# Eight token blocks instead of seven in the first feed-forward layer: 2, 2, 2, 3, 3, 4, 4, 4 chunks for 2, 2, 4, 4, 4, 4, 4

## The chip, the cores and the metric

The kernel runs on one core of one Trainium2 chip. The metric is the device time of one execution in microseconds, and the number quoted for a kernel is the median of several runs. Engines are named as in the profile: PE is the matmul engine and PEld its weight loads, DVE the vector engine, ACT the scalar engine, POOL GpSimd, SP the queue that issues the transfers.

## What is computed

A chunked linear-attention layer (4 batches, 8 heads, 768 positions, head dimension 32, state 16), then two feed-forward layers on the 3072 resulting tokens of width 256:

```python
y   = linear_attention(x, a, B, C)                 # a decaying state is carried along the positions
x1  = (sigmoid(y @ w_gate) * (y @ w_val)) @ w_out  # d_ff 1536: "layer 1"
h   = x1 @ w2_in                                   # d_ff 2048: "layer 2"
out = (h * sigmoid(h)) @ w2_out
```

All arrays are float32.

## The kernel before, in words

**Chunks.** The positions are cut into chunks of 128: six for each batch, 24 in all, numbered 0 to 23. One attention chunk `q` goes through the following steps. The loads `at_load_bc` (L265, L266), `at_load_x` (L273) and `at_loadL` (L252: 512 KB of decays, broadcast out of the small DRAM copy `ac_d`) are issued by SP. `at_bc1`, `at_bc2` and `at_bc3` split B and C in three bf16 parts and transpose them by DMA (L327). `at_L` is one long DVE scan over the decays (L338). `at_cb` multiplies C with B on PE (L381) and masks the product into `L` on DVE (L383). `at_y` makes the chunk's output in PSUM: four matmuls from the carried state (L392, none for the first chunk of a batch) and sixteen small ones (L398). `at_bw`, `at_cwT`, `at_state` and `at_state2` carry the state on (L346, L360, L414, L423, L435). `at_yT` writes the chunk into the block's input as a high part `xT0` (ACT, L450) and a low part `xT1` (DVE, L451). `y` has one PSUM buffer, `x` three buffers, `L` four, and each `xT` tile two. `slot_steps(s)` lists these steps for a slot `s`: the output of chunk `s`, the products of chunk `s + 1`, the preparation of chunk `s + 2` and the loads of chunk `s + 3`.

**Blocks and ticks.** Layer 1 takes the tokens in blocks of the chunks listed in `BLOCKS`; a block of `n` chunks is a moving operand of 128 `n` columns (256 for two chunks, 512 for four). A tick is a pair of a block and one of the twelve slices `f` of d_ff. A tick has six matmuls for the gate and six for the value (`three`, L509: two halves of the contraction by three products of high and low parts), a sigmoid out of PSUM on ACT (L522), the product out of PSUM on DVE (L530), the split into `gh` (ACT, L503) and `gl` (DVE, L539), and, two ticks later (`LAG`), six matmuls of `m1_out` (L558) that accumulate into `acc`. The gate and value products share three PSUM buffers (`gv`). At the end of a block `acc` is copied to `x1T` by two ACT copies (L569). Blocks 0 and 1 use the first seven `w_out` slices unsplit and have fewer, slower output matmuls there.

**Order.** Blocks 0 and 1 run interleaved, in groups of three slices, while the weights of layer 1 arrive and are split (`conv`). Their 24 ticks also work through a list of attention steps: all of what block 1 still needs, and the slots that fill block 2. From block 2 on the ticks are block by block, and the ticks of block `b` carry the slots of the chunks of block `b + 1`:

```python
ast += slots(ends[1] - 3, ends[1], ends[1], NQ) + slots(ends[1], ends[2], 0, NQ)
...
if b + 1 < len(BLOCKS):
    steps += [g for s in range(ends[b], ends[b + 1]) for g in slot_steps(s)]
    if b == 4:
        extra = w2_steps(0, NA)      # first weights of layer 2
```

`RUNS` and `WPOS` say how many of these steps stand before, between and behind the gate and the value of each of the 24 first ticks, and where the weight steps stand in the list. From block 2 on, a tick takes `rate` steps at each of three places, with `rate = -(-len(steps) // 32)`. SP issues its transfers in the order of the program. On the other engines the order is set when the kernel is built: the tile framework takes, by a simulated clock, the first instruction in program order that is ready. At run time each engine works through its own list in order.

**Where each chunk's block input lives.** Block 2 writes into the `xT` buffers of block 0, so that its first chunk (4) can be written only after the last gate and value of block 0 in slice 11; chunk 5's output waits for chunk 4's PSUM buffer, and so on.

Of the kernel before, what the change touches and what calls it, by code (L numbers as in the profile page):

```python
# [17 lines left out]
U32 = mybir.dt.uint32  # L18


BLOCKS = [2, 2, 4, 4, 4, 4, 4]
LAG = 2

NX = 4
# [21 lines left out]
def tile_linattn_moe_moe(  # L46
# [36 lines left out]
    U = nb * H  # L83
    assert sum(BLOCKS) == NQ and H * N == P and DM == 2 * P

# [131 lines left out]
    def w1_split(f0, f1):  # L217

        for f in range(f0, f1):
            hi, lo = w1[:, f, 0, 2 * DM :], w1[:, f, 1, 2 * DM :]  # L220
            nc.scalar.copy(hi, whole(f))
            nc.vector.tensor_sub(lo, whole(f), hi.bitcast(F32))
# [12 lines left out]
    blk_of = []  # L235
    for b, n in enumerate(BLOCKS):
        for i in range(n):
# [259 lines left out]
    g1 = {}  # L497
    start_of = [sum(BLOCKS[:b]) * L for b in range(len(BLOCKS))]

# [14 lines left out]
    def m1_gate(b, f):  # L514
        n = BLOCKS[b] * L
        ps = ps_gv.tile([P, 512], F32, tag="gv", name=f"g{b}_{f}", bufs=GV)
        three(ps, w1[:, f], 0, xT[b], n)
        if b < 2 and f < NAT:
            sg = gp.tile([P, 512], F32, tag=("gh", "gl")[f % 2], name=f"sg{b}_{f}", bufs=3)
        else:  # L520
            sg = gp.tile([P, 512], F32, tag="sg", name=f"sg{b}_{f}", bufs=2)
        nc.scalar.activation(sg[:, :n], ps[:, :n], AF.Sigmoid)  # L522
        g1[b, f] = [sg]

    def m1_val(b, f):
        n = BLOCKS[b] * L
        ps = ps_gv.tile([P, 512], F32, tag="gv", name=f"v{b}_{f}", bufs=GV)
        three(ps, w1[:, f], DM, xT[b], n)
        sg = g1[b, f][0]
        nc.vector.tensor_mul(sg[:, :n], ps[:, :n], sg[:, :n])  # L530
        if b >= 2 or f >= NAT:
            g1[b, f] += gsplit(f, sg, n, f"{b}_{f}")

    def m1_lo(b, f):
        n = BLOCKS[b] * L
        if len(g1[b, f]) == 1:
            return
        sg, hi, lo = g1[b, f]
        nc.vector.tensor_sub(lo[:, :n], sg[:, :n], hi[:, :n].bitcast(F32))  # L539

    def m1_out(b, f):
        n = BLOCKS[b] * L

        small = n <= 256
        if f == 0 and not (small and b % 2):
            acc[b] = ps_acc.tile([P, KM, 512], F32, tag="acc", name=f"acc{b}")
        a_ = acc[b - b % 2][:, b % 2] if small else acc[b]
        g = g1.pop((b, f))
        w = w1[:, f, :, 2 * DM :]
        if len(g) == 1:  # L550
            terms = ((whole(f), g[0]),)
        else:
            terms = ((w[:, 0], g[1]), (w[:, 0], g[2]), (w[:, 1], g[1]))
        for m in range(KM):
            ms = slice(m * P, (m + 1) * P)
            o = a_[:, m * n : (m + 1) * n] if small else a_[:, m, :n]
            for z, (v, g) in enumerate(terms):
                mm = nc.tensor.matmul(  # L558
                    o, v[:, ms], g[:, :n],
                    start=(f == 0 and z == 0 and not (small and m)),  # L560
                    stop=(f == NF1 - 1 and z == len(terms) - 1), skip_group_check=True,
                )
                if (b, f, m, z) in ZO:
                    pe_last[0] = mm.ins
                    zeros(ZO[b, f, m, z], o, False)
        if f == NF1 - 1:
            for m in range(KM):
                o = a_[:, m * n : (m + 1) * n] if small else a_[:, m, :n]
                x1_end[:] = [nc.scalar.copy(x1T[0][:, m, start_of[b] : start_of[b] + n], o)]  # L569
# [99 lines left out]
    def run(k):  # L669
        for _ in range(min(k, len(steps))):  # L670
            steps.pop(0)()

    def need(k):
        while k not in seen:
            steps.pop(0)()
# [5 lines left out]
    def w2_alloc(key, n):  # L681
        stack, side = (ctx, "left") if key == "a" else (w1stack, "right")
        w2p = stack.enter_context(tc.tile_pool(name=f"w2{key}", bufs=1, side=side))
        w2st[key] = w2p.tile([P, n, 2, 2 * DM], F32R, name=f"w2{key}")
# [13 lines left out]
    for b, f in ticks:  # L698
        if b < 2:
            need(("w", f))  # L700
            need(("x", b))
            z = f // GRP
            if b == 0 and f == z * GRP and z > 1:
                if (z - 2) * GRP < NAT:
                    steps.append(lambda z=z: w1_split((z - 2) * GRP, min((z - 1) * GRP, NAT)))
            if f == 0 and b == 1:
                rate = -(-len(steps) // RT)
        elif f == 0:
            run(len(steps))
            if b == 2:  # L710
                m1_lo(*prev)
                prev = None
                while queue_o:
                    m1_out(*queue_o.pop(0))
                for z in range(max(0, len(GR) - 2), len(GR)):
                    if z * GRP < NAT:
                        steps.append(lambda z=z: w1_split(z * GRP, min((z + 1) * GRP, NAT)))
                run(len(steps))
                sstack.close()
                w2_alloc("a", NA)  # L720
                stg["n"], stg["raw"], stg["cvt"] = 512, 2, 2
                stg["p"] = sstack.enter_context(tc.tile_pool(name="stg2", bufs=1))
            if b + 1 < len(BLOCKS):
                steps += [g for s in range(ends[b], ends[b + 1]) for g in slot_steps(s)]
                if b == 4:
                    extra = w2_steps(0, NA)
                    k = len(steps) // (len(extra) + 1)
                    for z, g in enumerate(extra):
                        steps.insert((z + 1) * (k + 1) - 1, g)
            else:  # L730
                astack.close()
                w2_alloc("b", NF2 - NA)
                held += w2_steps(NA, NF2)
            rate = -(-len(steps) // RT)
        counts = RUNS[ticks.index((b, f))] if b < 2 else [rate] * 3
        if b or f:
            run(counts[0])
        m1_gate(b, f)
        run(counts[1])
        if prev is not None:  # L740
            m1_lo(*prev)
        m1_val(b, f)
        prev = (b, f)
        run(counts[2])
        queue_o.append((b, f))
        if len(queue_o) > LAG:
            m1_out(*queue_o.pop(0))
        if held and f == LAG - 1:

            stg["behind"] = x1_end[0].ins  # L750
            steps += held
            held = []
            rate = -(-len(steps) // (3 * (NF1 - LAG)))
# [149 lines left out]
```

## Time and profile before

| | |
|---|---|
| median of 3 runs | 665.57 us (664.33 to 668.0) |
| the profiled execution, its own time | 663.99 us |
| span of its records | 662.2 us |
| mean granted PE clock | 0.992 of full speed |
| PE busy, weight loads busy | 635.5 us (96%), 522.0 us (79%) |
| DVE, ACT, POOL busy | 432.8 us (65%), 329.0 us (50%), 108.7 us (16%) |

The ends of matmuls are modelled in the trace, and one matmul's record overlaps the next. So a busy PE is not a PE at its peak: the distance from the start of one matmul to the start of the next says what it costs. A row of a timeline gives the start, the time from the start of the first to the end of the last instruction that it merges, and the idle time ahead of it with the instruction that ended it. Layer 1's blocks end, one after the other, with the two copies of L569; the last 264 us are layer 2.

### The profile page before, as it was taken

The page shows a single profiled execution, that of the slowest core. Times are in us where ns is not written, and L with a number is a line of the kernel's source. Part 1 is how long each engine was busy: PE and PEld are TensorE (multiplying, and loading weights), DVE is VectorE, ACT ScalarE, POOL GpSimd, SP SyncE. Part 2 cuts the span into 40 slices and gives each one's busy share as a digit, 9 for nine tenths or more (in the row PEclk, how much of TensorE's full clock was granted, in tenths as well). Part 3 has the DMA queues.
Part 4 walks back from the last instruction along what each step waited for, and adds up shares of the span by engine and source line. Part 5 has one row for each costly group of instructions (what it writes and reads, how often), then busy time and mean ns, then how long its engine had stood idle before and what let it go on. Part 6 is the DMA issues. An engine that isn't in the chain of part 4 may idle for free.

```text
span 662.2 us, 9861 instructions
## 1 busy us (share of the span) xinstructions
PE 635.5 (96%) x3680; PEld 522.0 (79%) x3682; DVE 432.8 (65%) x660; ACT 329.0 (50%) x649; POOL 108.7 (16%) x129
## 2 busy tenths in 40 slices
PE   5788898999999999999999999999999999999998
PEld 2477796777778787787888878888888888888886
DVE  8988987676768578656348885564564655544644
ACT  5675554544544554434336664544554544444543
POOL 4555432211221222311002410000000000000000
PEclk9998999999999999999999999999999999999999
DMA  8958577774656365342002410000000000000000
GB/s 207 267 146 212 89 158 154 153 128 109 120 121 145 77 145 119 81 125 75 0 1 66 157 33 1 1 32 1 1 32 1 1 32 1 33 0 1 33 0 33
DMA packets 140145, 51.18 MB, mean 77 GB/s; under 512 B 119009, under 2 KB 133537, under 8 KB 140097
## 3 DMA queue, kind: packets, MB, share of 16 engines
q1 hardware_dynamic: 139952, 50.41, 32.1%
q8 instruction: 29, 0.48, 0.3%
q14 instruction: 20, 0.16, 0.1%
q10 hardware_dynamic: 144, 0.13, 0.1%
HBM read 36.80 MB, written 3.24 MB: 60 GB/s over the span
## 4 chain that ended last, share of the span: by engine, by line
PE 79%; DVE 4%; DMA 4%; issue 3%; POOL 2%; ACT 1%; SPq 0%; DVEq 0%; POOLq 0%; ACTq 0%
PE h L509 20%; PE o L807 13%; PE v L509 11%; PE acc L558 11%; PE g L509 11%; PE o L828 7%; DMA raw<-in_moe_w_out_dram 3%; PE y L398 2%; DMA L<-ac_d 1%; POOL cvt L185 1%; PE cb L381 1%; PE y L392 1%; DVE sg L530 1%; DVE cvt L178 1%; DVE L L338 1%
## 5 line engine op out<-in xcount | busy, mean ns | idle before, releaser
L509 PE MATMUL v<-xT,w 128*128 128x512 f32 (+1 forms) x504 | 119.4, 369 | 3.9 <-ACT sg L522 2.4
L509 PE MATMUL g<-xT,w 128*128 128x512 f32 (+1 forms) x504 | 120.8, 370 | 0.0
L782 DVE TENSOR_TENSOR sh<-h,sh 128x512 f32<-128x512 f32 x96 | 66.2, 691 | 63.2 <-ACT sh L781 61.7
L509 PE MATMUL h<-x2T,w2b 128*128 128x512 f32 x432 | 107.0, 389 | 0.0
L791 DVE TENSOR_TENSOR gl<-sh,gh 128x512 fp32r<-128x512 f32 x96 | 65.8, 690 | 58.4 <-ACT gh L786 56.9
L509 PEld LDWEIGHTS v<-xT,w 128*128 128x128 f32 x504 | 87.4, 192 | 19.3 <-ACT sg L522 3.0
L509 PEld LDWEIGHTS g<-xT,w 128*128 128x128 f32 x504 | 87.7, 191 | 16.3 <-issue 1.5
L558 PE MATMUL acc<-gh,w 128*128 128x512 f32 (+1 forms) x280 | 94.5, 380 | 0.2 <-ACT x1T L569 0.2
L781 ACT ACTIVATE sh<-h 128x512 f32<-128x512 f32 x96 | 57.5, 599 | 73.3 <-PE h L509 70.2
L509 PEld LDWEIGHTS h<-x2T,w2b 128*128 128x128 f32 x432 | 80.7, 188 | 16.5
L786 ACT CAST gh<-sh 128x512 fp32r<-128x512 f32 x96 | 59.0, 620 | 62.2 <-PE o L807 31.0
L503 ACT CAST gh<-sg 128x512 fp32r<-128x512 f32 (+1 forms) x70 | 41.2, 588 | 93.6 <-DVE sg L530 93.6
L807 PE MATMUL o<-w2b,gh 128*128 128x512 f32 x280 | 74.2, 390 | 0.0
L530 DVE TENSOR_TENSOR sg<-v,sg 128x512 f32<-128x512 f32 (+1 forms) x84 | 50.8, 607 | 30.4 <-PE v L509 29.5
L539 DVE TENSOR_TENSOR gl<-sg,gh 128x512 fp32r<-128x512 f32 (+1 forms) x70 | 50.6, 723 | 23.3 <-ACT gh L503 23.0
L338 DVE TENSOR_TENSOR_SCAN L<-L,eye 128x1024 f32<-128x1024 f32 x24 | 55.2, 2302 | 16.0 <-DMA L<-ac_d 15.9
L185 POOL TENSOR_TENSOR cvt<-cvt,raw 128x512 int32<-128x512 int32 (+1 forms) x28 | 46.5, 1664 | 98.7 <-DVE cvt L178 81.5
L522 ACT ACTIVATE sg<-g 128x512 f32<-128x512 f32 (+1 forms) x84 | 44.8, 534 | 31.5 <-PE g L509 28.6
L558 PEld LDWEIGHTS acc<-gh,w 128*128 128x128 f32 x280 | 52.3, 190 | 9.9 <-ACT x1T L569 0.3
L807 PEld LDWEIGHTS o<-w2b,gh 128*128 128x128 f32 x280 | 51.8, 188 | 10.3
L558 PE MATMUL acc<-gl,w 128*128 128x512 f32 (+1 forms) x140 | 53.3, 380 | 1.0 <-DVE gl L539 1.0
L828 PEld LDWEIGHTS o<-w2b,gl 128*128 128x128 f32 x288 | 36.9, 191 | 1.3
(95 smaller groups left out, 724.9 us busy)
## 6 DMA issues: line engine op xcount, KB each, us to landing
L<-ac_d SPq DMA_DIRECT2D x23, 512.0 KB, 4.7
raw<-in_moe_w_out_dram SPq DMA_DIRECT2D x28, 256.0 KB, 3.9
raw<-in_moe_w_in_dram SPq DMA_DIRECT2D x16, 256.0 KB, 2.8
x<-in_x_dram SPq DMA_DIRECT2D x24, 128.0 KB, 3.1
raw<-in_moe_w_gate_dram SPq DMA_DIRECT2D x12, 256.0 KB, 4.4
raw<-in_moe_w_val_dram SPq DMA_DIRECT2D x12, 256.0 KB, 4.7
out_dram<-o2t SPq DMA_DIRECT2D x20, 128.0 KB, 1.7
bc<-in_B_dram SPq DMA_DIRECT2D x24, 64.0 KB, 2.7
```

The costliest lines, as they stand in the source:

```text
L185: nc.gpsimd.tensor_tensor(ti, ti, r, ALU.add)
L338: nc.vector.tensor_tensor_scan(t["Lf"], t["Lf"], eye, 0.0, op0=ALU.mult, op1=ALU.add)
L509: nc.tensor.matmul(psum[:, :n], w[:, i, o + k * P : o + (k + 1) * P], xt[j][:, k, :n], start=(z == 0), stop=(z == len(k_terms) - 1),)
L530: nc.vector.tensor_mul(sg[:, :n], ps[:, :n], sg[:, :n])
L539: nc.vector.tensor_sub(lo[:, :n], sg[:, :n], hi[:, :n].bitcast(F32))
L558: mm = nc.tensor.matmul(o, v[:, ms], g[:, :n], start=(f == 0 and z == 0 and not (small and m)), stop=(f == NF1 - 1 and z == len(terms) - 1 ...
L781: nc.scalar.activation(sg, ps, AF.Sigmoid)
L782: nc.vector.tensor_mul(sg, ps, sg)
L786: nc.scalar.copy(hi, sg)
L791: nc.vector.tensor_sub(lo, sg, hi.bitcast(F32))
L807: nc.tensor.matmul(ps, hi[:, s], w2(f)[:, :, DM:], start=(f == 0), stop=False, skip_group_check=True,)
L828: nc.tensor.matmul(ps[:, :DM], g2[b, f][2][:, s], w2(f)[:, 0, DM:], start=False, stop=(f == NF2 - 1), skip_group_check=True,)
```

## The change

`BLOCKS` has eight entries in place of seven. Blocks 0 and 1 stay as they are. The old blocks 2 and 3 (chunks 4 to 7 and 8 to 11) become three: block 2 with chunks 4 and 5, block 3 with 6 to 8, block 4 with 9 to 11. The last three blocks keep their chunks and get the numbers 5 to 7; the second edit keeps the loading of the first layer-2 weights in the block that holds chunks 12 to 15. The list of attention steps that the 24 first ticks carry gets shorter by two slots, since it ends where block 2 is filled (`ends[2]` is 6 in place of 8); `RUNS` and `WPOS` are as before.

```diff
-BLOCKS = [2, 2, 4, 4, 4, 4, 4]
+BLOCKS = [2, 2, 2, 3, 3, 4, 4, 4]
 LAG = 2
...
                 steps += [g for s in range(ends[b], ends[b + 1]) for g in slot_steps(s)]
-                if b == 4:
+                if b == 5:
                     extra = w2_steps(0, NA)
                     k = len(steps) // (len(extra) + 1)
                     for z, g in enumerate(extra):
```

## Rows read from the trace of the kernel before

**Rows 1.** The page: weight loads of the value product; xcount, busy, mean ns, idle before.

```profile
L509 PEld LDWEIGHTS v<-xT,w 128*128 128x128 f32 x504 | 87.4, 192 | 19.3 <-ACT sg L522 3.0
```

**Rows 2.** Busy time by stage; from,to, five engines with instructions, clock, DMA.

```profile
core 0: us, PE busy (x) PEld busy (x) DVE busy (x) ACT busy (x) POOL busy (x), PEclk, DMA share, GB/s
...
40.00:97.00 57.00, 49.58 (x363) 45.10 (x362) 51.40 (x74) 34.57 (x71) 28.46 (x26) 0.94 0.66 149
97.00:112.50 15.50, 12.91 (x151) 10.86 (x150) 11.94 (x23) 6.54 (x20) 2.89 (x6) 1.00 0.71 147
112.50:180.00 67.50, 67.50 (x427) 52.62 (x425) 47.79 (x74) 30.79 (x67) 14.46 (x25) 1.00 0.66 133
```

**Rows 3.** The chain that ended last, 93 to 110 us; start, us, what.

```profile
93.43 4.94 DMA L<-ac_d
...
98.39 2.30 DVE L L338
...
102.88 4.25 DMA L<-ac_d
...
109.36 0.41 DVE xT L451
```

**Rows 4.** PE in order of time, 99 to 113 us.

```profile
99.43 0.64 PE L398 MATMUL y<-L,x 128*32 128x128 f32 x16
...
101.33 0.32 PE L414 MATMUL st<-x,bw 128*32 128x64 f32 x8 [0.82 <-POOL bw L346]
...
104.32 0.65 PE L398 MATMUL y<-L,x 128*32 128x128 f32 x16
...
109.81 0.71 PE L392 MATMUL y<-cwT,S 128*128 128x128 f32 x4 [1.61 <-DVE xT L451]
...
112.49 0.47 PE L509 MATMUL g<-xT,w 128*128 128x512 f32 x1
```

**Rows 5.** PE's matmuls by shape, 97 to 112.5 us; xcount, busy, mean ns.

```profile
L558 PE MATMUL acc<-gh,w 128*128 128x256 f32 x20 | 4.6, 292 | 0.2 <-ACT x1T L569 0.2
L509 PE MATMUL v<-xT,w 128*128 128x256 f32 x18 | 3.1, 295 | 0.0
L558 PE MATMUL acc<-gl,w 128*128 128x256 f32 x10 | 3.0, 301 | 0.0
L509 PE MATMUL g<-xT,w 128*128 128x256 f32 x12 | 2.6, 308 | 0.0
L398 PE MATMUL y<-L,x 128*32 128x128 f32 x48 | 2.1, 281 | 0.0
L381 PE MATMUL cb<-tr,tr 128*128 128x128 bf16 x16 | 1.6, 222 | 0.0
```

**Rows 6.** ACT in order of time: the copies that end blocks 2, 3, 5, 6.

```profile
179.96 1.07 ACT L569 COPY x1T<-acc 128x512 f32<-128x512 f32 x2
237.11 1.07 ACT L569 COPY x1T<-acc 128x512 f32<-128x512 f32 x2
...
349.25 1.07 ACT L569 COPY x1T<-acc 128x512 f32<-128x512 f32 x2
398.23 1.08 ACT L569 COPY x1T<-acc 128x512 f32<-128x512 f32 x2 [0.25 <-PE acc L558]
```

**Rows 7.** PE in order of time, 91 to 92 us: matmuls of 256 columns.

```profile
91.05 0.88 PE L509 MATMUL g<-xT,w 128*128 128x256 f32 x6
91.77 0.88 PE L509 MATMUL v<-xT,w 128*128 128x256 f32 x6
```

**Rows 8.** DVE in order of time: two scans and what each waited for.

```profile
98.39 2.29 DVE L338 TENSOR_TENSOR_SCAN L<-L,eye 128x1024 f32<-128x1024 f32 x1 [0.95 <-DMA L<-ac_d]
...
107.15 2.29 DVE L338 TENSOR_TENSOR_SCAN L<-L,eye 128x1024 f32<-128x1024 f32 x1 [0.78 <-DMA L<-ac_d]
```

**Rows 9.** SP in order of time: the B loads of two chunks that follow each other.

```profile
99.78 0.53 SPq L265 DMA_DIRECT2D bc<-in_B_dram  x1
...
108.39 0.53 SPq L265 DMA_DIRECT2D bc<-in_B_dram  x1
```

## The prediction

> **What bounds the kernel now.** I read the page first, then the busy time by stage [rows 2]. From 112.5 us on PE has no idle time that the trace records in layer 1's full blocks (67.50 of 67.50 us). Before that it has some: 49.58 of 57 us busy between 40 and 97 us, with DVE at 51.40, and 12.91 of 15.5 us between 97 and 112.5 us. The reader is to see three stages: a start in which the weights arrive and are split, a seam of 15.5 us, and then PE alone.
>
> What a saturated PE costs is read from distances. The last layer-1 block carries no attention; its end stands 48.98 us behind the end of the block before (398.23 - 349.25) [rows 6]. That is 12 ticks of 18 matmuls of 512 columns, so 48.98 / 216 = 0.227 us each. A matmul of 256 columns costs 0.120 us: six of the gate start 0.72 us ahead of the six that follow [rows 7]. A straight line through the two has 0.107 us per 256 columns and a fixed part of 0.120 - 0.107 = 0.013 us for each matmul. Block 3 with four chunks of attention under it took 57.15 us (237.11 - 179.96) [rows 6]; less 48.98 that is 8.2 us, so a chunk costs PE 2.04 us.
>
> Then I read the seam. Its matmuls are 60 of 256 columns (20 + 18 + 10 + 12), 48 of `y`, which is three chunks' worth, and 16 of `cb`, two chunks' worth [rows 5]. By the prices above that is 60 x 0.120 = 7.2 us, plus two chunks at 2.04 us, plus a third `y` at 0.6 us [rows 4], plus about 0.1 us of the first 512-column matmul: 12.0 us of work in 15.5 us. So 3.5 us of PE time are lost there. PE's own list names the larger holes: 0.82 us until POOL had made `bw`, and 1.61 us until DVE had written `xT` [rows 4]. The chain of waits says what is behind both: twice a transfer of `L` (4.94 and 4.25 us), then the scan on it, then, in DVE's queue behind the second scan, chunk 6's `xT` [rows 3]. The full blocks start at 112.49 us [rows 4], when chunk 7 is written.
>
> **The change part by part.** *The start, up to about 100 us: nothing.* The list of steps keeps its first part. What falls off its end are the output of chunks 6 and 7, the products of 7 and 8, and the preparation of 8 and 9. Written out from the code, the list is 90 attention steps long for 124 before, all of the weight steps stand inside the 90, and the 24 ticks take the same steps at the same places until it ends in tick (0, 5). The earliest work in the seam that belongs to the removed part is the state product at 101.33 us [rows 4]. The lists are made greedily by a clock, so that leaving out later work changes nothing ahead of it.
>
> *The seam: -3.0 us.* Block 2 now needs only chunks 4 and 5. The `y` at 99.43 us is chunk 5's, the one at 104.32 chunk 6's, the one at 109.81 chunk 7's [rows 4]; so chunk 5 can be written some two microseconds after 100 us. Some 46 of the 60 small matmuls are left after 100 us, 5.5 us of work, and PE can fill gaps between them with block 2's gates. So the last work of blocks 0 and 1 ends near 105.5 us, and block 2 starts at about 104 to 106 us rather than at 112.49. The 7 us in between are not gained: the attention work that stood in them, 3.5 us, moves into the blocks. What is gained is the idle PE, at most 3.5 us, at least nothing (if the holes come from blocks 0 and 1 themselves). I take 3.0: the two named holes belong to chunks 7 and 6, which leave, and half a microsecond stays for the last ticks' chain of sigmoid, product, split and output.
>
> *The blocks: +2.9 us.* Twenty-four ticks of 512 columns become 12 of 256 and 24 of 384. The columns are the same. The matmuls are 36 x 18 = 648 for 432, so 216 more, at 0.0133 us each: 2.9 us, all of it on a saturated PE. For 384 columns the trace has no row; the line gives 0.173 us. The bounds: if 384 columns cost in proportion to 512 (0.170 us), only the 256-column block pays, 216 x 0.120 - 108 x 0.227 = 1.4 us; if a matmul of 384 columns cost as much as one of 512, 0.227 us, the 432 of them would add (0.227 - 0.173) x 432 = 23 us more. I take the line, 2.9: at the two widths that the rows show, the distance follows the columns, with nothing that looks like a step, and so I keep the upper end out of the range.
>
> One rule of the Trainium skill is weighed here. The rows put the fixed part of a matmul at 0.013 us [rows 6, 7]. The page "TensorE: Matmul & The Clock Gate", section "Back-to-back issue gap", gives the warm gap as the columns over 2.4 GHz and 2.5 ns more; by that the 216 matmuls would cost an estimated 0.5 us, and the sum below would be 2.4 us lower. The trace does not bear it out: 512 columns would take 0.216 us by it, and they take 0.227.
>
> *Block 2's narrow ticks: +1.5 us.* The ticks of block 2 hold 18 x 0.120 = 2.2 us of matmuls; with three chunks of attention the block takes 25.9 + 6.1 = 32 us. Two things get tighter. First the three product buffers: between the end of a value and the gate after next, which needs that buffer, stand a gate, a value and one output group, 18 x 0.120 = 2.2 us, and up to 0.6 us of attention. DVE must free the buffer in that time, and a scan that waits for its decays holds DVE for 0.95 + 2.29 or 0.78 + 2.29 us [rows 8]. That is 0.3 to 1.0 us too long for each of three chunks. In the old 512-column ticks the same distance is 4.1 us, and the hole is covered. Second the loads: SP issues a chunk's B load 8.61 us after that of the chunk before (108.39 - 99.78) [rows 9], since the transposes of one chunk stand between. Block 2 asks for a chunk in about 17 steps, which at 6 steps a tick and 2.8 us a tick is 7.9 us, somewhat faster than SP gave in the seam. Bounds: nothing, if the order that the simulated clock finds puts the products ahead of the scans; three times the loss of the seam for each of its two chunks (3.5 / 2 = 1.75), 5.2 us. I take 0.5 us for each of three chunks, 1.5 us. Blocks 3 and 4 have 18 x 0.173 = 3.1 us in that distance, and their chunk comes every 8 to 10 us: nothing there.
>
> *What stays.* DVE and ACT get twelve ticks more of four short instructions, hidden under PE. There is one block end more. Block ends at 512 columns cost PE nothing that the trace shows. Blocks 5 to 7 are the old 4 to 6, with the layer-2 weights under the same chunks, and layer 2 is untouched.
>
> **The sum.** -3.0 + 2.9 + 1.5 = +1.4 us. Against the profiled execution's own 663.99 us (a span of 662.2 and 1.8 around it) that is 665.4. The median of the runs stands 1.6 us above that execution, at 665.57 us, so I predict a median of 667.0 us.
>
> **The rivals.** *Slower: block 2 stalls as the seam does.* If the waits of the seam only move into block 2, each of its three chunks costs 1.75 us of idle PE: -3.0 + 2.9 + 5.2 = +5.1 us, 670.7. It decides from the point where a scan with its wait holds DVE longer than the 2.2 to 2.8 us between a value and the gate that needs its buffer. For it: the waits of 0.78 and 0.95 us [rows 8]. Against: between 91 and 92.5 us matmuls of 256 columns ran back to back [rows 7], with the weights' splitting still on DVE. Chance 0.22.
>
> *The change does not do what it says: the seam keeps its holes.* Blocks 0 and 1 may hold PE up by their own last products, or block 2 may wait for chunk 5. Then nothing is gained: +2.9 us and up to 1.5, so 668.5 to 670, say 669. Against: both named holes are of later chunks. Chance 0.13.
>
> *Faster: no new stall, and 384 columns in proportion.* -3.5 + 1.4 = -2.1 us, 663.5. For it: the full blocks show no idle PE at all [rows 2]. Against: the fixed part is plain at two widths. Chance 0.08.
>
> *The weight loads come into the open.* Every matmul has a load, of 192 ns on the mean [rows 1], longer than the 120 ns of 256 columns; were the 216 new ones not covered, they would add 216 x 0.192 = 41 us, 708. Against: the matmuls of 256 columns start 0.120 us apart with such loads between them [rows 7], so loads overlap matmuls and each other. Chance 0.01. The same page states, in "The mechanism" of its part on packing small matmuls, that a load overlaps a matmul in flight only where the row group differs; these loads are all of 128 rows, and the trace does not agree: 0.120 us leaves no room for an uncovered load.
>
> The forecast has the remaining 0.56.
>
> **How the numbers follow.** The forecast alone reaches from -1 us (no stall in block 2, all idle time gained) to +3 us: 664.5 to 668.5. The slower rival and the one without a gain hold 0.35 and lie mostly below 671, so the range goes to 671.0; at the lower end 663.0 takes in the faster rival. About 0.15 are left out, most of it above. 0.5% of the median, about what can be told from no change, is 3.3 us: faster means below 662.2, slower above 668.9. Slower takes most of the first rival (0.18), half of the second (0.07) and a little of the forecast and the rest (0.03): 0.28. Faster takes a small part of the faster rival and of the forecast: 0.05. The rest is 0.67.
>
> **What the profile after would show.** Right: the first 384-column gate about 0.173 us apart; the first matmuls of block 2 at 104 to 106 us; no hole over 0.5 us in PE between 101 and 106 us; in block 2 some holes ended by DVE's product or by the sigmoid, 1.5 us together; the last copies of layer 1 near 399.6 us in place of 398.23. Wrong: holes in the seam that name DVE or ACT work of blocks 0 and 1; a distance other than 0.170 to 0.174 us at 384 columns; more than 3 us of idle PE in blocks 2 to 4; any difference before 97 us.

## The result: 673.21 us for 665.45

The changed kernel takes 673.21 us (672.47 to 673.43, four runs) beside 665.45 us of the kernel before in the same session: a ratio of 1.0118, interval 1.0083 to 1.0154. That is 7.8 us slower, where 1.4 us were forecast, and outside the range. The profiled execution took 673.28 us with a span of 671.6 us, 9.4 us longer than before. (The profiled execution of before, 663.99 us, stands 1.5 us below its median, so the two traces lie 1.5 us further apart than the medians.)

All of it is lost in layer 1. Its last copies start at 407.55 us in place of 398.23 [rows 6], 9.3 us later, and what follows lasts 264 us in both. ACT in order of time, the copies that end the blocks of the changed kernel:

```profile
105.41 0.64 ACT L569 COPY x1T<-acc 128x256 f32<-128x256 f32 x2
...
113.43 0.65 ACT L569 COPY x1T<-acc 128x256 f32<-128x256 f32 x2
...
153.54 0.64 ACT L569 COPY x1T<-acc 128x256 f32<-128x256 f32 x2
...
198.74 0.86 ACT L569 COPY x1T<-acc 128x384 f32<-128x384 f32 x2
...
246.05 0.85 ACT L569 COPY x1T<-acc 128x384 f32<-128x384 f32 x2
...
303.83 1.07 ACT L569 COPY x1T<-acc 128x512 f32<-128x512 f32 x2
...
357.73 1.07 ACT L569 COPY x1T<-acc 128x512 f32<-128x512 f32 x2
407.55 1.08 ACT L569 COPY x1T<-acc 128x512 f32<-128x512 f32 x2 [0.25 <-PE acc L558]
```

From the end of block 1 to the end of chunk 11's block are 246.05 - 113.43 = 132.62 us; the same chunks took 237.11 - 112.56 = 124.55 us. That stretch alone has lost 8.1 us. Block 1 ends 0.9 us later (113.43 for 112.56, one of ACT's copies in the trace of before); the last three blocks together lose 0.4 us.

Next, the busy time by stage (from:to, then PE, PEld, DVE, ACT and POOL with their instructions, the clock, the DMA share and GB/s), of the changed kernel:

```profile
40.00:97.00 57.00, 48.94 (x357) 44.17 (x356) 51.18 (x73) 33.28 (x69) 28.42 (x26) 0.94 0.62 146
97.00:112.50 15.50, 14.94 (x144) 13.06 (x147) 10.95 (x21) 6.49 (x20) 2.21 (x5) 1.00 0.74 139
112.50:140.00 27.50, 25.89 (x249) 22.78 (x249) 20.72 (x42) 13.72 (x41) 8.91 (x14) 1.00 0.67 144
140.00:200.00 60.00, 59.70 (x441) 54.74 (x441) 35.58 (x62) 23.66 (x57) 6.87 (x12) 1.00 0.52 89
200.00:408.00 208.00, 206.98 (x1193) 169.69 (x1193) 140.38 (x220) 104.78 (x207) 45.46 (x46) 1.00 0.37 91
```

and one row of the kernel before, for the stretch behind that of [rows 2]:

```profile
200.00:398.50 198.50, 197.48 (x1083) 158.50 (x1082) 133.39 (x202) 99.59 (x189) 40.96 (x38) 1.00 0.34 86
```

PE's recorded idle time in the seam fell from 15.50 - 12.91 = 2.59 us [rows 2] to 0.56 us. But 27.50 - 25.89 = 1.61 us stand between 112.5 and 140 us, where there was none, and 0.30 us more up to 200 us; behind 200 us it is 1.02 us in both. Idle time moved, 2.03 us out of the seam and 1.91 us into blocks 2 and 3. It doesn't explain 9.3 us.

PE in order of time in the changed kernel, block 2's first gate and its neighbours, then the larger holes:

```profile
104.76 0.43 PE L398 MATMUL y<-L,x 128*32 128x128 f32 x8
105.11 0.98 PE L509 MATMUL g<-xT,w 128*128 128x256 f32 x6
106.02 0.41 PE L398 MATMUL y<-L,x 128*32 128x128 f32 x2
106.36 0.39 PE L558 MATMUL acc<-gh,w 128*128 128x256 f32 x1
106.58 0.28 PE L558 MATMUL acc<-gl,w 128*128 128x256 f32 x1
...
108.22 0.42 PE L398 MATMUL y<-L,x 128*32 128x128 f32 x6
108.57 0.98 PE L509 MATMUL v<-xT,w 128*128 128x256 f32 x6
...
110.59 0.39 PE L558 MATMUL acc<-gh,w 128*128 128x256 f32 x1 [0.56 <-ACT gh L503]
...
128.55 0.40 PE L381 MATMUL cb<-tr,tr 128*128 128x128 bf16 x4 [1.02 <-DVE L L383]
...
135.87 0.98 PE L509 MATMUL g<-xT,w 128*128 128x256 f32 x6 [0.59 <-DVE sg L530]
...
162.56 0.42 PE L558 MATMUL acc<-gh,w 128*128 128x384 f32 x1
162.82 0.34 PE L558 MATMUL acc<-gl,w 128*128 128x384 f32 x1
...
163.69 1.20 PE L509 MATMUL g<-xT,w 128*128 128x384 f32 x6
164.73 1.20 PE L509 MATMUL v<-xT,w 128*128 128x384 f32 x6
```

Two things are to be seen beside the holes. A chunk's `y` is sixteen records of L398, from eight float32 matmuls that leave two records each (and the four records of L392 are two matmuls). Chunk 6's lie in three pieces, of 8, 2 and 6, with gates and output matmuls between. These take 0.35, 0.34 and 0.35 us up to the next matmul, almost whatever is in them. And the first layer-1 matmul behind a piece is long. The six gates from 105.11 take 0.91 us up to 106.02, where six of 256 columns take 0.72 us [rows 7]; `acc` from 106.36 lasts 0.22 us for 0.12, and `acc` from 162.56 0.26 us where 384 columns take (164.73 - 163.69) / 6 = 0.173. Counted through, chunk 12's records even lie in five pieces:

```profile
170.32 0.42 PE L398 MATMUL y<-L,x 128*32 128x128 f32 x6
...
178.53 0.41 PE L398 MATMUL y<-L,x 128*32 128x128 f32 x2
...
179.24 0.41 PE L398 MATMUL y<-L,x 128*32 128x128 f32 x4
...
182.91 0.41 PE L398 MATMUL y<-L,x 128*32 128x128 f32 x2
...
188.50 0.41 PE L398 MATMUL y<-L,x 128*32 128x128 f32 x2
```

In the kernel before chunk 12's is one piece (at 168.66 us). A whole `y` looks like this there, 0.57 us from its start to the next matmul:

```profile
204.02 0.64 PE L398 MATMUL y<-L,x 128*32 128x128 f32 x16
204.59 0.33 PE L360 MATMUL cwT<-ident,cw 128*128 128x128 f32 x1
```

**A ledger of PE.** From the starts of all matmuls between 97 us and layer 1's last output matmul I took each distance from one layer-1 matmul to the next, less 0.0133 us and 0.107 us per 256 columns. What is left falls into classes. A *group* is attention work between two layer-1 matmuls; the *way back* is the excess of the matmul right behind a group (where it also stands ahead of the next group, it counts there). Idle time is what the trace records as such.

| | before | after | more |
|---|---|---|---|
| groups of attention on PE | 49 | 67 | 18 |
| of them with `y` matmuls of L398 | 26 | 33 | 7 |
| time of the groups without idle time (us) | 33.32 | 35.26 | +1.9 |
| excess of the matmul ahead of a group (us) | 2.14 | 3.42 | +1.3 |
| way back (us) | 4.43 | 5.95 | +1.5 |
| recorded idle time (us) | 3.6 | 3.5 | -0.1 |
| smaller gaps (us) | 0.9 | 1.9 | +1.0 |
| the layer-1 matmuls by that line (us) | 252.2 | 255.9 | +3.7 |
| layer 2's first matmuls among them (us) | 4.1 | 4.1 | 0 |

The third to fifth lines are what attention costs PE: 39.9 us before and 44.6 us after, 4.7 us more. The layer-1 line holds the 216 matmuls' fixed part, 2.9 us, and 0.8 us of seven more matmuls that were still to come at 97 us. Of the smaller gaps' 1.0 us, 0.8 stand in the last block, which carries no attention; there they come to 0.4 to 1.2 us in the traces of the other runs, so they may be the execution's. The sum is 9.3 us.

### The profile page after: what moved, and what is told of

It reads as the page before. It is cut to its first block, busy times and chain, and to the rows that moved or that the text cites. A ratio compares the mean times of both kernels' runs of the same rounds, so it can differ in the third digit from the quotient of the medians.

```text
span 671.6 us, 10364 instructions
## 1 busy us (share of the span) xinstructions
PE 647.8 (96%) x3898; PEld 544.6 (81%) x3898; DVE 434.4 (65%) x684; ACT 330.1 (49%) x675; POOL 109.4 (16%) x129
## 4 chain that ended last, share of the span: by engine, by line
PE 73%; DMA 6%; DVE 4%; issue 3%; ACT 3%; SPq 2%; POOL 2%; ACTq 0%; DVEq 0%; POOLq 0%
PE h L509 19%; PE o L807 13%; PE acc L558 10%; PE v L509 10%; PE g L509 10%; PE o L828 7%; DMA raw<-in_moe_w_out_dram 3%; DMA L<-ac_d 2%; PE y L398 2%; POOL cvt L185 2%; SPq L327 1%; PE cb L381 1%; DVE sg L530 1%; PE y L392 1%; ACT cvt L175 1%
## 5 line engine op out<-in xcount | busy, mean ns | idle before, releaser
L509 PE MATMUL v<-xT,w 128*128 128x256 f32 (+2 forms) x576 | 122.8, 345 | 4.4 <-ACT sg L522 2.8
L509 PE MATMUL g<-xT,w 128*128 128x256 f32 (+2 forms) x576 | 124.3, 348 | 1.1 <-DVE sg L530 0.9
L509 PEld LDWEIGHTS g<-xT,w 128*128 128x128 f32 x576 | 95.4, 192 | 14.1 <-DVE sg L530 2.7
L558 PE MATMUL acc<-gh,w 128*128 128x512 f32 (+2 forms) x328 | 100.2, 351 | 0.6 <-ACT gh L503 0.6
L503 ACT CAST gh<-sg 128x512 fp32r<-128x512 f32 (+2 forms) x82 | 43.5, 531 | 98.0 <-DVE sg L530 97.8
L530 DVE TENSOR_TENSOR sg<-v,sg 128x256 f32<-128x256 f32 (+2 forms) x96 | 52.6, 549 | 34.6 <-PE v L509 33.9
L539 DVE TENSOR_TENSOR gl<-sg,gh 128x512 fp32r<-128x512 f32 (+2 forms) x82 | 51.7, 631 | 31.5 <-ACT gh L503 31.3
L558 PEld LDWEIGHTS acc<-gh,w 128*128 128x128 f32 x328 | 60.2, 190 | 7.5 <-ACT gh L503 1.2
L522 ACT ACTIVATE sg<-g 128x256 f32<-128x256 f32 (+2 forms) x96 | 46.9, 490 | 27.9 <-PE g L509 25.6
L558 PE MATMUL acc<-gl,w 128*128 128x512 f32 (+2 forms) x164 | 57.5, 350 | 1.0 <-DVE gl L539 1.0
```

What stands on the lines that cost most here:

```text
L509: nc.tensor.matmul(psum[:, :n], w[:, i, o + k * P : o + (k + 1) * P], xt[j][:, k, :n], start=(z == 0), stop=(z == len(k_terms) - 1),)
L558: mm = nc.tensor.matmul(o, v[:, ms], g[:, :n], start=(f == 0 and z == 0 and not (small and m)), stop=(f == NF1 - 1 and z == len(terms) - 1 ...
```

## The experiments

Three theories stood at the outset. A: beside the fixed part, PE idles 4 to 5 us, because narrow ticks under attention at full pace cover its waits less. B: the shorter list upsets the seam, and the narrow ticks cost only their fixed part. C: a narrow tick costs much more than its fixed part wherever it stands. "Before" is the kernel before in the same session. The experiments came in five lots.

**Narrow blocks away from the seam.** The change's sizes, with the three short blocks late:

```diff
-BLOCKS = [2, 2, 2, 3, 3, 4, 4, 4]
+BLOCKS = [2, 2, 4, 4, 3, 3, 2, 4]
-                if b == 5:
+                if b == 4:
```

> Blocks of 2, 2, 4, 4, 3, 3, 2 and 4 chunks: as many ticks of 256, 384 and 512 columns as the change has, but the narrow ones come late, when the seam and the fast attention behind it are over; the list of steps for the first 24 ticks stays as long as before. Theory A (2.9 us of fixed cost for 216 more matmuls, wherever they stand, and some 4 to 5 us of idle PE because the narrow ticks of the change run under attention at full pace and cover its waits less): the kernel before + 2.9 us + up to 1.5, so +3 to +4.5 us. Theory B (the loss comes of the shorter list, which reorders the seam; narrow ticks cost only their fixed part): +2.9 us. Theory C (a narrow tick costs much more than its fixed part wherever it stands): about +8 us, as the change.

Measured: 676.76 us for 664.4, ratio 1.0176 (1.0147 to 1.0206), +12.4 us. ACT's copies show the start as it was in [rows 6], and the loss behind it:

```profile
180.20 1.06 ACT L569 COPY x1T<-acc 128x512 f32<-128x512 f32 x2
...
238.05 1.07 ACT L569 COPY x1T<-acc 128x512 f32<-128x512 f32 x2
...
410.27 1.07 ACT L569 COPY x1T<-acc 128x512 f32<-128x512 f32 x2 [0.26 <-PE acc L558]
```

From 238.05 to 410.27 are 172.2 us, where before has 161.1: 11.1 us, and 2.9 of them are the fixed part. So narrow ticks cost far more than the fixed part in a place that has no seam. A (+3 to +4.5 us) and B (+2.9) fall as the whole cause; C fits in kind, though the loss is above its 8 us. The ledger finds 73 groups in this run, 39 with `y`, and attention costs PE 6.8 us more than before.

**Threes.** Four blocks of 384 columns, and none of 256 behind the first two:

```diff
-BLOCKS = [2, 2, 2, 3, 3, 4, 4, 4]
+BLOCKS = [2, 2, 3, 3, 3, 3, 4, 4]
```

> Blocks of 2, 2, 3, 3, 3, 3, 4 and 4 chunks: again 216 more matmuls than before, but no 256-column block behind the seam; the list of steps ends one slot earlier than before, not two. Theory A: the fixed 2.9 us, and less idle time than in the change, since a tick of 384 columns covers 3.1 us of a scan and its wait and one of 256 only 2.2: +3.5 to +5.5 us. Theory B: 2.9 and half of the rest, since the list is cut by half as much: +5 us. Theory C: as the change, +7 to +8 us.

Measured: 675.79 us, ratio 1.0173 (1.0146 to 1.02), +11.4 us, though it too adds only 216 matmuls. PE's large holes in the seam, in order of time, are those of [rows 4] again:

```profile
100.44 0.32 PE L414 MATMUL st<-x,bw 128*32 128x64 f32 x8 [0.67 <-POOL bw L346]
105.79 0.39 PE L558 MATMUL acc<-gh,w 128*128 128x256 f32 x1 [0.34 <-ACT x1T L569]
109.44 0.71 PE L392 MATMUL y<-cwT,S 128*128 128x128 f32 x4 [1.61 <-DVE xT L451]
```

A block 2 of three chunks keeps the seam as it was, so the change's two chunks do shorten these holes. Groups number 71, those with `y` 36; attention costs 7.6 us more than before, and the recorded idle time ahead of groups and in them is 4.3 us, for 2.6 before. (The granted clock was 0.95 and 0.96 in this profile between 97 and 140 us, so its seam is read for the order of the waits and not for tenths, and part of the 7.6 us may be the clock's.)

**The list of the first ticks kept long.** The change's blocks, with the attention list as long as before:

```diff
-    ast += slots(ends[1] - 3, ends[1], ends[1], NQ) + slots(ends[1], ends[2], 0, NQ)
+    ast += slots(ends[1] - 3, ends[1], ends[1], NQ) + slots(ends[1], 8, 0, NQ)
...
-                steps += [g for s in range(ends[b], ends[b + 1]) for g in slot_steps(s)]
+                steps += [g for s in range(max(ends[b], 8), ends[b + 1]) for g in slot_steps(s)]
```

> The blocks of the change, but the first 24 ticks keep the list of the kernel before (the slots up to 8), and the later blocks take the slots from there on: widths alone. Theory A: as the change, +7 to +9 us. Theory B: the seam's order is that of before again, so only the 2.9 us of the widths stay: +3 us.

Measured: 672.91 us, ratio 1.0117 (1.0092 to 1.0143), the change's own time. Theory B falls: what the list holds at its end doesn't matter for the time. Attention costs 5.3 us more than before here.

**Twos.** The old block 2 alone cut in two, no 384-column block:

```diff
-BLOCKS = [2, 2, 2, 3, 3, 4, 4, 4]
+BLOCKS = [2, 2, 2, 2, 4, 4, 4, 4]
```

> Blocks of 2, 2, 2, 2, 4, 4, 4 and 4 chunks: 216 more matmuls again, but all the narrow ticks are of 256 columns and stand in blocks 2 and 3, under the attention at full pace; blocks 4 to 7 are as before. Theory A: the fixed 2.9 us and at least the idle time of the change: +8 to +11 us. Theory B: the same cut of the list as in the change, +7 to +8 us, with nothing more for the second narrow block. Theory that the blocks of three chunks are what costs: +3 to +4 us.

Measured: 672.0 us, ratio 1.011 (1.0086 to 1.0135), +7.6 us. So blocks of three chunks aren't what costs (+3 to +4 us by that theory). The ledger: 64 groups, 28 with `y`, attention 3.1 us dearer than before. The fixed part is the same 216 matmuls, but only four chunks lie in narrow blocks for the change's eight, and the loss is nearly the change's: what goes beyond the fixed part doesn't follow the narrow columns in proportion.

**PE in program order.** The second lot meant to take the number of groups away directly: attention at one place in a tick, PE held to the program's order from block 2 on, in the change and in the blocks of before.

```diff
+            if b == 2:
+                sp_order.enter_context(tc.manual_schedule(engines={mybir.EngineType.PE}))
-        counts = RUNS[ticks.index((b, f))] if b < 2 else [rate] * 3
+        counts = RUNS[ticks.index((b, f))] if b < 2 else [0, 0, 3 * rate]
```

> The blocks of the change; from block 2 on PE follows the program's order, and a tick takes its attention steps at one place, behind the value, in place of three. So the attention matmuls stand in fewer, longer groups: PE goes 44 times from layer-1 matmuls over to attention, against 83 times in the change and 65 in the kernel before. Theory D (beside the 2.9 us of fixed cost, the loss of the change is that its narrower ticks make the simulated clock cut the attention into more groups, and each group costs PE some 0.2 us, half of it behind the group's end): 39 groups fewer, about 8 us faster than the change, so about as fast as the kernel before. Theory A (the loss is waits of narrow ticks for DVE): no faster than the change, +7 to +9 us on the kernel before, or slower, since PE can no longer pass by what is not ready.

> The blocks of the kernel before, with the same two edits: PE in program order from block 2 on, a tick's attention steps at one place. 46 groups of attention against 65. Theory D: 19 groups fewer at 0.2 us, 3 to 4 us faster than the kernel before. Theory A: no gain, or a loss of some microseconds from waits that PE can't pass by.

Measured: 708.04 us, ratio 1.0653 (1.0625 to 1.0682), and 708.66 us, 1.0685 (1.0659 to 1.071). A miss: PE now stops at attention whose data is not there, `cb` behind DVE's mask alone 13.1 us in 13 places in the first and 17.0 us in the second. What it tells is that attention at one place and in a fixed order costs over 40 us; the price of a group it doesn't tell.

**The price of a group.** So the third lot added groups that wait for nothing to block 5 of the kernel before (chunks 16 to 19): thirty bf16 matmuls of zeros, 128 columns each, one at a time between output matmuls, and the same thirty in five runs of six. They accumulate zeros into `acc`.

```diff
+    ZO = {(5, f, m, z): 1 for f in range(6, 11) for m in range(2) for z in range(3)}   # thirty
+    ZO = {(5, f, 1, 2): 6 for f in range(6, 11)}                                        # five runs
...
+                    zeros(ZO[b, f, m, z], o[:, :P], False)
```

> The kernel before, with thirty small bf16 matmuls of 128 columns by zeros added in block 5, whose ticks 6 to 10 carry no attention: one behind each of the six output matmuls of a tick, in five ticks. Each is a group of its own. They add zeros to the sums. Theory D: each costs its 0.05 us and the 0.2 us of a group, 30 x 0.25 = 7.5 us, all between the end of block 4 and the end of block 5. If a change over to a small matmul and back is free: 30 x 0.053 = 1.6 us.

> The same thirty small matmuls in the same ticks of block 5, but six behind each other behind the last output matmul of a tick: five groups in place of thirty. Theory D: 1.6 us of matmuls and 5 x 0.2 us, 2.6 us. If each small matmul costs what it costs wherever it stands: the same as with thirty groups.

Measured: 667.87 us, ratio 1.0058 (1.0041 to 1.0075), and 667.15 us, 1.0047 (1.0029 to 1.0064). PE in order of time in the first:

```profile
331.66 0.23 PE L143 MATMUL acc<-zz 128*128 128x128 bf16 x1
331.70 0.48 PE L558 MATMUL acc<-gl,w 128*128 128x512 f32 x1
332.02 0.23 PE L143 MATMUL acc<-zz 128*128 128x128 bf16 x1
332.06 0.48 PE L558 MATMUL acc<-gh,w 128*128 128x512 f32 x1
```

A pair takes 0.36 us, of which 0.227 are the 512 columns: 0.133 us for a single group, where such matmuls start 0.055 us apart in the runs of six. The rest, 0.08 us, stands in the matmul that follows. Block 5 agrees: 57.78 us for 53.78 in the kernel before (its copies start at 295.47 and 349.25), 4.0 us for thirty; the five runs cost 1.85 us, 0.37 each, of which six matmuls are 0.33. So a group costs some 0.04 to 0.08 us beyond its matmuls, well under the 0.2 us of theory D, and eighteen more of them 1.4 us at most. By the medians the two runs lie 3.7 and 3.0 us above before and their intervals overlap, so this price rests on one trace of each.

**Whole and cut `y`.** Next the same for what `y` is made of: forty matmuls of zeros in float32, 32 columns of weights, in five groups of eight, and in twenty groups of two.

```diff
+    def tiny(n, o, i0):
+        ...
+                nc.tensor.matmul(o[p : p + 32, :P], z4[:, :32], z4[:, :P], start=False, stop=False, ...)
+    ZO = {(5, f, 1, 2): (8, 0) for f in range(6, 11)}                                              # whole
+    ZO = {(5, f, m, z): (2, 4 * m + z) for f in range(6, 11) for m in range(2) for z in (0, 2)}    # cut
```

> The kernel before, with forty small float32 matmuls like those of y (32 weight columns, 128 moving columns, by zeros, so that they add nothing) in ticks 6 to 10 of block 5, which carry no attention: eight behind each other at the end of a tick's output group, five groups. Theory E (a group of y matmuls costs PE some 0.35 us to begin, 0.02 us for each of its two-pass halves and 0.09 us for the way back to layer 1, so that cutting a group in two costs 0.4 us): 5 x (0.35 + 16 x 0.022 + 0.09) = 4.0 us more than before. Theory that each small matmul has its price wherever it stands: this run gives that price, and the next one shows the same.

> The same forty small matmuls in the same ticks, but two behind each other, four times in a tick's output group: twenty groups in place of five. Theory E: 20 x (0.35 + 4 x 0.022 + 0.09) = 10.6 us more than before, 6.6 more than whole groups. If only the way back costs (0.09 us): 15 x 0.09 = 1.4 us more than whole groups. If cutting is free: as the whole groups.

Measured: 670.1 us, ratio 1.0083 (1.0056 to 1.011), and 676.23 us, 1.0177 (1.0149 to 1.0204). PE in order of time, whole (each such matmul leaves two records):

```profile
331.76 0.39 PE L567 MATMUL acc<-gh,w 128*128 128x512 f32 x1
332.08 0.64 PE L152 MATMUL acc<-zz 128*32 128x128 f32 x16
332.65 1.21 PE L518 MATMUL g<-xT,w 128*128 128x512 f32 x4
```

and cut:

```profile
333.51 0.39 PE L567 MATMUL acc<-gh,w 128*128 128x512 f32 x1
333.83 0.41 PE L152 MATMUL acc<-zz 128*32 128x128 f32 x4
334.17 0.50 PE L567 MATMUL acc<-gl,w 128*128 128x512 f32 x1
334.51 0.40 PE L567 MATMUL acc<-gh,w 128*128 128x512 f32 x1
```

Sixteen records take 0.57 us as `y` does, four still take 0.34 us, and the matmul on either side is 0.09 to 0.11 us longer than 0.227. Block 5 took 58.10 us with whole groups and 64.99 us with cut ones: 6.9 us for fifteen more groups and the same forty matmuls (6.1 by the medians, 6.6 by theory E), 0.46 us for a cut. This is the first price that is large enough to matter. A cut into halves of eight records costs less, 2 x 0.35 - 0.57 = 0.13 us and the long matmuls on either side.

**No cuts, two ways.** The fourth lot tried to take the cuts out of the change. First a chunk's `y` as one piece that PE may not leave, from chunk 6 on, in the change and in the blocks of before:

```diff
+        with tc.tile_critical() if crit else nullcontext():
+            for pt in parts:                 # both halves of y, one behind the other
```

> The blocks of the change, but the sixteen y matmuls of a chunk from chunk 6 on are marked as one piece that the simulated clock can't cut (the slots from 6 on use the joint form for it). In PE's list there are 25 groups with y matmuls, against 39 in the change, and 81 groups of attention in all against 84. Theory E: 14 groups at 0.35 to 0.45 us, 4 to 6 us faster than the change, so +2 to +4 us on the kernel before. If the loss is the waits of narrow ticks: as the change, +8 us.

> The blocks of the kernel before with the same y in one piece: 25 groups with y matmuls against 32, but 75 groups of attention in all against 66. Theory E: 7 x 0.35 less, 9 x 0.09 more, 1 to 2 us faster than before. If the groups cost nothing: no difference, or slower by waits of a piece that can't be passed.

Measured: 695.35 us, ratio 1.0456 (1.043 to 1.0483), and 682.76 us, 1.0272 (1.025 to 1.0294). A miss as the program order was: such a piece holds PE also for work of other engines that its matmuls don't read, in the first for 5.4 us in three places for POOL's `bcr`.

Then by priority: `y` goes ahead of other ready work, alone or with both its halves in one step, from chunk 4 on; the last of the three is the joint one with the blocks of before. The edit shown is the joint one.

```diff
+        joint = q >= 4
+        if joint and part == 0:
+            return
+        with tc.high_priority() if q >= 4 else nullcontext():
+            for pt in (1, 0) if joint else (part,):
```

> The change, with one edit: the y matmuls of chunks 4 and later have the highest priority for the simulated clock, so that a layer-1 matmul that becomes ready doesn't come between them. In PE's list 28 groups with y matmuls in place of 39, 81 groups of attention in all in place of 84. Theory E (each cut of a y group costs about 0.46 us, as thirty and five groups of dummy matmuls showed): 11 groups fewer, some 5 us faster than the change, so +2 to +4 us on the kernel before. Theory A (waits of narrow ticks for DVE): as the change, +7 to +8 us.

> The change with the same priority, and both halves of a chunk's y behind each other from chunk 4 on, the half that is ready later first. 24 groups with y matmuls in place of 39, but 86 groups in all in place of 84, so 17 more without y. Theory E: 15 x 0.46 less, 17 x 0.09 more, some 5 us faster than the change, +2 to +4 us on the kernel before. Theory A: as the change, +7 to +8 us.

> The kernel before with the same two edits as the run before this one: 24 groups with y matmuls in place of 32, 79 groups in all in place of 66, so 21 more without y. Theory E: 8 x 0.46 less and 21 x 0.09 more, 1 to 3 us faster than the kernel before. If only the groups in all counted: about 1 us slower.

| | median | ratio | groups, with `y` | groups and matmul ahead | idle at groups | way back |
|---|---|---|---|---|---|---|
| the kernel before | 665.45 | 1 | 49, 26 | 35.5 | 2.6 | 4.43 |
| the change | 673.21 | 1.0118 (1.0083 to 1.0154) | 67, 33 | 38.7 | 1.3 | 5.95 |
| priority | 672.03 | 1.0108 (1.0082 to 1.0134) | 64, 22 | 36.5 | 3.2 | 5.85 |
| joint | 670.16 | 1.0078 (1.0049 to 1.0107) | 69, 19 | 34.6 | 2.2 | 6.04 |
| joint, old blocks | 665.31 | 1.0015 (0.9999 to 1.0031) | 62, 19 | 33.9 | 3.4 | 5.60 |

(The table counts from 97 us on, the expectations in PE's whole list.) The cuts go and their work with them, 2.1 and 4.1 us; in the joint form attention costs PE 40.7 us, near the 39.9 of before, though the groups in all are not fewer. But `y` that may not be cut waits at its group, 1.9 and 0.9 us more. A cut is partly how PE fills such a wait, so that only 0.7 and 2.7 us come back by the ratios, whose intervals overlap the change's. In the old blocks the same edit gives nothing that can be told from no change.

**The decays first.** Last the waits: in the seam each scan waits for its transfer of `L` [rows 8], the last of a chunk's loads. The slot's load of `L` put ahead of its transposes, in the blocks of before and in the change:

```diff
         add(s, at_yT)
+        if s >= 1:
+            add(s + 3, at_loadL)
         add(s + 2, at_bc3, 0)
...
-            add(s + 3, at_loadL)
```

> The blocks of before, with each chunk's load of the decays L put ahead of its transposes and its loads of B and C. Theory late L (the scans of the seam end late because L is asked for after B, C and x): the two holes of the seam, 0.82 and 1.61 us, shrink, and the time falls by 1 to 2.5 us to about 662 to 663.5. Theory pace (the holes come from how the attention steps lie on PE and the vector engine): within 1 us of before.

> The change's blocks, with the same edit. Theory late L: waits between layer 1's matmuls fall from 2.9 us to about 1, and the time falls by about 2 us to 671. Theory pace: within 1 us of the change, 672 to 674; the groups stay near 67 and so does their cost.

Measured: 672.08 us for 664.5, ratio 1.0118 (1.0093 to 1.0143), and 678.53 us, 1.0206 (1.0182 to 1.023): 7.6 us slower than before and 5.3 us slower than the change; neither theory foretold a loss. PE's holes in the seam, old blocks:

```profile
107.66 0.38 PE L381 MATMUL cb<-tr,tr 128*128 128x128 bf16 x4 [1.30 <-DVE sg L531]
110.51 0.39 PE L559 MATMUL acc<-gh,w 128*128 128x256 f32 x1 [1.00 <-ACT x1T L570]
115.56 1.20 PE L392 MATMUL y<-cwT,S 128*128 128x128 f32 x4 [2.71 <-DVE xT L451]
```

and two of SP's rows there:

```profile
101.53 4.31 SPq L327 DMA_TRANSPOSE tr<-st  x2
105.95 0.53 SPq L265 DMA_DIRECT2D bc<-in_B_dram  x1
```

The tenth scan starts at 102.71 us in place of 107.15 [rows 8], so `L` did come earlier. But the B load that stood at 99.78 [rows 9] is now at 105.95, with the transposes ahead of it, and the `xT` of 109.36 us [rows 3] is written at 115.00. The holes grew from 2.4 to 5.0 us. Behind them the granted clock fell to 0.71 between 112 and 120 us, so partly to the lower of its two levels, and 0.89 up to 130, where it is 1.00 before ([rows 2], from 112.5 us on); ahead of that PE had been busy in 5.61 of the 8 us from 104. So part of this run's loss is the clock's. In the changed blocks it stayed at 1.00. The theory of the late `L` falls as the sole cause, and that of the pace, which had the time unchanged within 1 us, isn't borne out either. What is early on SP's queue makes something else late here, and a chunk still comes every 8 to 10 us.

## Why the prediction was wrong

**The step that failed** is the price of attention inside the blocks. "A chunk costs PE 2.04 us" was read from a full block of 512 columns and carried over, so that the part on the blocks had only the fixed part of 216 matmuls, and the sum no term for how PE's list lies. Blocks 3 and 4 of the change show it. Block 3 took 198.74 - 153.54 = 45.20 us, its 216 matmuls of 384 columns 37.4, and the three chunks whose `y` lies in it (11 to 13) the other 7.8: 2.6 us each. Block 4 has 8.3 us beside its layer-1 matmuls for three chunks (14 to 16), 2.8 each. Read in the same way, blocks 2 to 4 of the kernel before have 2.1 to 2.3. Over the whole stretch, with eighteen more groups in PE's list, that is 3.2 us in the groups and the matmuls ahead of them and 1.5 us of way back: 4.7 us that the sum lacked. The pieces' prices are measured apart (0.04 to 0.08 us for a short group, 0.34 us at least for one of `y`). Taking cuts away took most of the work away in the trace and part of the time, not all. Why the list made at build time cuts more when ticks are narrow I have not shown; fewer columns leave more places at which an attention step is the first that is ready, which would do it.

**The seam, -3.0 us:** half right, and undone. The term was above the 2.59 us of idle time that [rows 2] record there. That idle time fell by 2.0 us, and block 2's first gates start at 105.11 us, within the forecast 104 to 106. But the step said that the attention of chunks 6 and 7 would move into the blocks and the last work of blocks 0 and 1 end near 105.5 us. Chunk 7's `y` did move, to 115.0 us from 110.5, but chunk 6's stands at 104.76 for 104.32, and block 1 ended at 113.43. SP, in order of time, issued the B loads of the changed kernel

```profile
100.12 0.53 SPq L265 DMA_DIRECT2D bc<-in_B_dram  x1
...
109.50 0.53 SPq L265 DMA_DIRECT2D bc<-in_B_dram  x1
```

where before has 99.78 and 108.39 [rows 9], and DVE's scans came at 98.53 and 107.50 us for 98.39 and 107.15. The transfers and scans kept their calendar though the steps stood further down the list. PE used the time for block 2: 94 layer-1 matmuls stand between 97 us and block 1's end, for 59 before. (That block 1 ends 0.9 us later says little: in the traces of the four runs with zeros in block 5, whose first part is that of before, it ends at 112.11 to 116.02 us.)

**Block 2's narrow ticks, +1.5 us:** near. The recorded idle time in blocks 2 and 3 is 1.9 us, ended as foretold by DVE's product (0.59 us at 135.87), but also by the mask `L` (1.02 us at 128.55); in the seam `gh` ended 0.56 us (at 110.59). Taken with the seam the forecast was a gain of 1.5 us; the idle time of the ledger came out at 0.1 us less. This is the second miss, 1.4 us, most of it the seam's. The rival "block 2 stalls as the seam does" named the move of the waits, 2.0 us out of the seam and 1.9 into blocks 2 and 3, but had 5.2 for it. Neither it nor the forecast had a term for dearer attention, which alone is more than half of the 7.9 us between the forecast +1.4 and the traces' +9.3.

**The fixed part, +2.9 us:** right. 384 columns take 0.173 us, as the line gave, and the ledger has 2.9 us for the 216. The Trainium skill's page "TensorE: Matmul & The Clock Gate", section "Back-to-back issue gap", gives the columns over 2.4 GHz and 2.5 ns, an estimate of 0.1625 us here; the trace doesn't agree with it at this width either. The weight loads stayed covered: at 0.120 and 0.173 us apart there is no room for one of 190 ns.

**The start, nothing:** right within 0.8 us. PE has six matmuls fewer behind it at 97 us (357 for 363), 0.64 us by its busy time, though the order of its matmuls is the same up to there. Executions differ by more: 555 matmul records lie ahead of 97 us in the trace of before, 550 in the change's, and 546, 540, 556 and 561 in those of the four runs with zeros in block 5.

**What stays open.** The ledger's waits and cuts can't be fully parted, since the runs without cuts waited more. No run parted the waits of blocks 2 and 3 from their cause; the decays' run only excludes the simplest one. None of the versions beat the kernel before.

## What to carry to other kernels

Price a narrower tile by its fixed part per instruction, and then ask what lies between the tiles: where another stream is woven in, more and shorter pieces of that stream can cost more than the fixed part (here 4.7 us beside 2.9). Count the pieces, price the shortest one by itself, and don't carry a price of the woven stream from wide tiles over to narrow ones. Idle time in a seam isn't gained for good by asking for less work there when something else sets the pace at which that work comes: here the loads of the seam kept their times to within 1.1 us, the idle time came back in the blocks behind, and moving one load ahead made the others late.

## What the runs showed of the hardware

A group of other matmuls between 512-column ones costs time that isn't in its own records (the granted clock was 1.00 in these stretches): the matmul behind it starts its successor 0.08 to 0.11 us late, whether the group has one bf16 matmul or sixteen fp32 records. In the two runs with small fp32 matmuls the one ahead of the group was 0.09 us long as well. And a group of fp32 matmuls with 32 columns of weights takes 0.34 us for two, 0.35 for six or eight and 0.57 for sixteen records: four records and eight cost the same, so there is a floor under a piece that its number of matmuls doesn't show.
